# Sparse attention and a top-2 mixture of experts: queries and keys laid out head dimension first, inputs as contiguous blocks, a third PSUM bank for P x V

## The chip, the core and the metric

The kernel runs on one core of one Trainium2 chip. A core has five engines that work side by side and wait for each other by semaphores: PE (TensorE, matmuls; its weight loads are shown as PEld), DVE (VectorE), ACT (ScalarE), POOL (GpSimd) and SP (SyncE, which here only issues DMAs). PE writes into PSUM, which has eight banks of 128 x 512 float32. The metric is device time in microseconds, the median of several runs. Host work in `kernel()` ahead of the launch is not in it.

## What is computed

```python
def _attn_ref(q, k, v, n_sink, window):              # 4 batches, 8 heads, 768 tokens, head dimension 64
    scores = scale * np.matmul(q, k.transpose(0, 1, 3, 2))
    is_sink = pos[None, :] < int(n_sink)             # n_sink = 4
    rel = pos[:, None] - pos[None, :]
    in_window = (rel >= 0) & (rel < int(window))     # window = 128
    scores = np.where(is_sink | in_window, scores, -1000000000.0)
    a = np.exp(scores - np.max(scores, axis=-1, keepdims=True))
    a = a / (np.sum(a, axis=-1, keepdims=True) + 1e-09)
    return np.matmul(a, v)

def _moe_ref(x, w_gate, w_noise, noise, w1, w2):     # 3072 tokens of 512, 8 experts of 1024
    noisy_logits = x @ w_gate + np.log1p(np.exp(x @ w_noise)) * noise
    top2 = np.argpartition(-noisy_logits, 2, axis=1)[:, :2]
    top2_w = ...
    for e in range(E):
        for k in range(2):
            mask = top2[:, k] == e
            h = np.maximum(x[mask] @ w1[e], 0.0)
            out[mask] += top2_w[mask, k, None] * (h @ w2[e])
```

Attention's output, 512 wide per token, is the x of the mixture.

## The kernel before

The program has two phases, and each is recorded into a planner (`Plan`) before it is built. Every piece of work is entered with its engine, a duration, a priority and the tiles that it reads and writes. `Plan.run` then plays the list through: each engine takes, of the pieces that are ready, the one with the smallest priority, and the order that comes out is the order in which each engine's instructions are built. Priorities are a tile number plus offsets from the table `PR`; other entries of `PR` choose engines (`dv_pool`, `pc_pool`, `cm_pool`). Rings (`plan.rings`) say how many buffers of a kind there are; a piece waits until the buffer of its number minus the ring's size is free. SP's DMA issues form one queue in the built order.

Phase one (L1186) is attention with routing woven in. 16 pairs of heads (`g`) with 3 tiles of 256 queries (`jj`) each make 48 tiles `n = 3 g + jj`. Per pair, `load_qk` (L259) brings keys and queries with tokens on partitions (`kn`, `qn`), in runs of 64 floats; for the first pair in three parts, later in one part of two DMAs each. `turn` (L276) lets PE transpose two key and two query blocks of 128 tokens (L280) into the PSUM tile `T`, `turn_c` (L286) copies it with ACT into `kq`, and `ksink` (L290) lets POOL copy the four sink keys beside each key block. `load_v` (L267) brings the values, and `dv` (L271, built by the helper at L192) takes the difference of neighbouring value blocks, on POOL for one pair in four and on DVE for the others.

Per tile: `qk` (L307) writes scores into `S`; ACT copies the previous key block (L310) and DVE merges the current one under a mask (L315, L317) into `cbuf`; DVE takes the maximum (L327), POOL subtracts it (L192), ACT takes exp (L334), DVE sums (L337) and inverts (L345). `ptr` (L365) transposes the probabilities on PE into `P`, ACT copies them to `CT` (L368), POOL or DVE masks them to `CM` (L377, L375). `pv` opens a PSUM tile `X`: a transpose of the sinks' probabilities (L382), values times `CT` (L388), differences times `CM` (L391); ACT copies the sinks' part (L395), `sinks` adds it (L400), ACT copies the result (L408), `rows` transposes it into the same `X` (L413), and DVE scales it into `xr` (L416), which SP stores to `x_rows` (L423). One X tile is thus in use from L382 to L416. The sinks' values come by 16 small DMAs per batch (L247) into a tile that POOL has cleared (L241). `logits` (L593, L601) and `routing` of a finished batch take X tiles of the same ring.

PSUM in phase one: `S` two tiles of two banks, `P` one, `T` one, `X` two. `T` serves the first expert's rows as well (L881). Phase two runs the last batch's routing and the experts: `up` (L997 to L999) and `down` (L1026 to L1032) on PE, weights by `w_chunk` (L918) through the tile `st`, `gather` on POOL, results added into `out` by POOL (L1050).

Of the kernel before, what the change touches and what calls it, by code (L numbers as in the profile page):

```python
# [9 lines left out]
F32 = mybir.dt.float32  # L10
# [29 lines left out]
def dram(t, off, ap):  # L40
    return bass.AP(tensor=t.tensor, offset=t.offset + off, ap=ap)
# [135 lines left out]

def constants(nc, pool, sh):
# [16 lines left out]
def attention(tc, plan, consts, cst, sh, q, k, v, xbuf):  # L195
# [6 lines left out]
    plan.rings.update(vr=2, kn=2, qn=2, vn=2, dv=2, skn=2, sqn=2, kq=2, C=5, mn=3, sm=4, ri=2, pc=3,  # L202
                      CT=2, CM=2, ps=3, xr=3, S=2, P=1, T=1, X=2, xtn=5, lt=1, lm=1, lg=2)
# [71 lines left out]

    def turn(g, gi, ti):  # L276
        p = get("T", ti, [128, 4, 128], F32, "ps")
        for x, nm in enumerate(("kn", "qn")):
            for a in range(2):
                nc.tensor.transpose(p[:, 2 * x + a, :], get(nm, g)[:, 2 * gi + a].rearrange("p h d -> p (h d)"), idf)  # L280

    def kq(g):
        return get("kq", g, [128, NJ, 4, KW])

    def turn_c(g, gi, ti):
        nc.scalar.activation(kq(g)[:, gi, :, NS:], get("T", ti), AF.Copy)  # L286

    def ksink(g, gi):
        t = kq(g)
        nc.gpsimd.tensor_copy(t[:, gi, :2, :NS], t[:, 0, 0:1, NS:2 * NS].to_broadcast([128, 2, NS]))  # L290
# [140 lines left out]
    def load(nm, g, gi, z):  # L431
        plan.dma(z, lambda: load_qk(nm, g, gi), 1.9 if gi is None else .65, w=[(nm, g, i) for i in parts(gi)], u=[(nm, g)], n=2)

    def parts(gi):
        return range(NJ) if gi is None else (gi,)

    def turns(g, gi, z):
        ti = plan.next("T")
        op("PE", .43, z + P(g, "tgroup"), lambda: turn(g, gi, ti), r=[(nm, g, gi) for nm in nms], w=[("T", ti)], u=[(nm, g) for nm in nms])
        op("ACT", .49, z + P(g, "tgroup_c"), lambda: turn_c(g, gi, ti), r=[("T", ti)], w=[("kq", g, gi)], u=[("kq", g)])  # L440
        op("Pool", .14, z + P(g, "ksink"), lambda: ksink(g, gi), r=[("kq", g, 0), ("kq", g, gi)], w=[("ks", g, gi)], u=[("kq", g)])
# [13 lines left out]
    for g in range(NP):  # L455
        p0 = g * NJ
        e = p0 - NJ
        for nm in nms:
            if g:
                load(nm, g, None, (g - 3) * NJ + PR.get("load_qk", 0) + 1.5 * (nm == "qn") if g > 1 else -18)  # L460
        if g:
            loads_v(g)
        for gi in range(NJ):
            turns(g, gi, e + PR.get("t0", .8) + PR.get("t2", .4) * gi)
            if g == 0 and gi == 0:
                plan.op("SP", 0, -19, None, r=[("kq", 0, 0), ("ks", 0, 0)], w=[("go", 0)], lat=0)
        if g == 0:
            loads_v(0)
# [9 lines left out]
        for jj in range(NJ):  # L478
# [31 lines left out]
            op("PE", .14, n + .6 + P(g, "sinks"), lambda n=n: sinks(n), r=[("ps", n), ("vr", g // HP)], w=[("X", xa)], kind=3)  # L510
# [8 lines left out]
def routing_setup(nc, pool, tmp, cst, sh, w_gate, w_noise, noise):  # L519
# [4 lines left out]
    wbd = c["wbd"] = tmp.tile([128, HP, 2, 2, E], F32, name="wbd")  # L524
    nc.gpsimd.memset(wbd, 0.0)
# [40 lines left out]
def gate_loads(nc, plan, cst, sh, w_gate, w_noise, noise):  # L566
    c, wbd = cst, cst["wbd"]
    D, E, HP, T = sh.D, sh.E, sh.H // 2, sh.T

    def load():  # L570
        for h in range(2):
            for i, w in enumerate((w_gate, w_noise)):
                nc.sync.dma_start(wbd[h * D:(h + 1) * D, :, h, i, :], dram(w, h * D * E, [[E, D], [2 * D * E, HP], [1, E]]))
        nc.sync.dma_start(c["nz"], dram(noise, 0, [[E, 128], [128 * E, T], [1, E]]))

    c["gates"] = lambda: plan.dma(2, load, 4, r=[("xrow", 0)], w=[("rc", 0)], n=5)
# [341 lines left out]
def w_chunk(plan, nc, sh, w1, w2, e, m, i, z, lo_eng="DVE", first=()):  # L918
# [4 lines left out]
    quarters = m == 1 and e > 0  # L923

    def load():
        t = get("st", n, [128, 1024], F32, "early")
        if m == 1:
            t = t.rearrange("p (k f) -> p k f", k=4)
            o = e * sh.DM * sh.F + i * 256
            if quarters:  # L930
                for q in range(4):
                    nc.sync.dma_start(t[32 * q:32 * q + 32], dram(w1, o + q * 128 * sh.F, [[sh.F, 32], [32 * sh.F, 4], [1, 256]]))
            else:
                nc.sync.dma_start(t, dram(w1, o, [[sh.F, 128], [128 * sh.F, 4], [1, 256]]))
        else:
# [367 lines left out]
```

## Time and profile before

| What | Value |
|---|---|
| Runs before | 839.18 us median of 3 (837.86 to 840.2) |
| Span of the profiled execution | 836.0 us (the page gives no time of it beside the span) |
| Granted TensorE clock, mean | 0.990 |
| DMA | 97.10 MB in 151750 packets, 100704 of them under 512 B |
| First H matmul of the experts | 226.89 us from the start |

The profile is of one execution. A table by stretch gives the busy time of each engine between two times; a row of the timeline gives start, length, engine, line and operation, with the idle time ahead of it and what ended that in brackets; a row of groups gives an operation's count, its busy time and mean length, and the idle time just ahead of it; a row of waits gives the total, the number of times and the longest. Most fp32 matmuls appear as two records each, transposes as one.

### The profile page before, as it was taken

What the parts mean: (1) busy time and instruction counts of PE and PEld (TensorE: products, weight loads), DVE (VectorE), ACT (ScalarE), POOL (GpSimd) and SP (SyncE); (2) the same over time, 40 slices, a digit from 0 to 9 for tenths busy, and PEclk for the clock granted to TensorE, in tenths of its full rate; (3) what the DMA queues carried; (4) which work ended last, traced back from release to release, by engine and by line L of the source; (5) the groups of instructions that cost most, each with busy time, mean ns of one, the idle gap of its engine ahead of it and who ended that gap; (6) DMA issues with size and microseconds to landing.
All of it is one profiled execution on the core that took longest, in us unless ns stands there. A gap on an engine that the chain in (4) does not pass through costs nothing.

```text
span 836.0 us, 13410 instructions
## 1 busy us (share of the span) xinstructions
PE 794.0 (95%) x4801; PEld 668.6 (80%) x4801; DVE 442.8 (53%) x1094; ACT 343.5 (41%) x677; POOL 430.3 (51%) x601
## 2 busy tenths in 40 slices
PE   6999997898899799999999999999999999999996
PEld 3776775676677589888988988898899889889984
DVE  5878979888673334346335424633542463454220
ACT  4876785675521323234233323423332341433210
POOL 6555866767416325472753647275364627526212
PEclk9999999999999899999999999999999999999999
DMA  6749886644544186175444617544461654444123
GB/s 120 154 96 226 181 204 183 157 127 100 141 132 131 31 224 165 29 152 120 94 84 127 136 31 153 122 92 84 129 131 35 150 124 94 80 130 78 21 31 47
DMA packets 151750, 97.10 MB, mean 116 GB/s; under 512 B 100704, under 2 KB 129376, under 8 KB 151680
## 3 DMA queue, kind: packets, MB, share of 16 engines
q1 hardware_dynamic: 137744, 67.93, 31.8%
q0 software_dynamic: 13936, 28.27, 19.4%
q8 instruction: 39, 0.64, 0.3%
q14 instruction: 31, 0.25, 0.1%
HBM read 67.44 MB, written 28.72 MB: 115 GB/s over the span
## 4 chain that ended last, share of the span: by engine, by line
PE 75%; issue 7%; DVE 6%; POOL 4%; DMA 4%; ACT 2%; another core or an unknown queue 1%; SPq 1%; POOLq 0%; DVEq 0%; ACTq 0%
PE H L997 10%; PE H L999 10%; PE H L998 10%; PE Y L1026 9%; PE Y L1028 9%; PE Y L1027 9%; PE S L307 4%; PE X L388 2%; PE T L280 2%; PE X L391 2%; POOL out L1050 2%; PE P L365 1%; PE Y L1031 1%; PE Y L1032 1%; DMA st<-in_moe_w 1%
## 5 line engine op out<-in xcount | busy, mean ns | idle before, releaser
L1050 POOL DMA_INDIRECT out<-y,idx x56 | 92.0, 1642 | 241.2 <-ACT y L1035 209.3
L838 POOL DMA_INDIRECT xg<-x_rows,rt_idq x182 | 180.6, 992 | 55.5 <-issue 53.4
L1015 DVE SCALAR_TENSOR_TENSOR h<-H,h 128x384 fp32r<-128x384 f32 (+2 forms) x192 | 79.4, 441 | 219.6 <-ACT h L1008 142.2
L997 PE MATMUL H<-skn,w 128*128 128x448 f32 (+3 forms) x512 | 181.6, 355 | 1.8 <-issue 1.8
L999 PE MATMUL H<-skn,w 128*128 128x448 f32 (+3 forms) x512 | 180.5, 353 | 1.5 <-issue 1.5
L998 PE MATMUL H<-sqn,w 128*128 128x448 f32 (+3 forms) x512 | 179.3, 350 | 1.8 <-issue 1.8
L1008 ACT ACTIVATE h<-H 128x448 fp32r<-128x448 f32 (+3 forms) x128 | 66.1, 516 | 273.7 <-PE H L999 161.8
L997 PEld LDWEIGHTS H<-skn,w 128*128 128x128 f32 x512 | 96.2, 188 | 11.2 <-issue 3.1
L998 PEld LDWEIGHTS H<-sqn,w 128*128 128x128 f32 x512 | 96.3, 188 | 10.6 <-issue 2.4
L999 PEld LDWEIGHTS H<-skn,w 128*128 128x128 f32 x512 | 96.3, 188 | 7.3 <-issue 1.8
L1026 PE MATMUL Y<-w2b,h 128*128 128x512 f32 x192 | 76.0, 396 | 0.3 <-ACT h L1008 0.2
L1028 PE MATMUL Y<-w2b,h 128*128 128x512 f32 x192 | 75.5, 393 | 0.5 <-DVE h L1015 0.5
L1026 PE MATMUL Y<-w2a,h 128*128 128x512 f32 x192 | 75.5, 393 | 0.0
L1027 PE MATMUL Y<-w2b,h 128*128 128x512 f32 x192 | 75.5, 393 | 0.0
L1027 PE MATMUL Y<-w2a,h 128*128 128x512 f32 x192 | 75.0, 391 | 0.0
L1028 PE MATMUL Y<-w2a,h 128*128 128x512 f32 x192 | 74.8, 389 | 0.0
L307 PE MATMUL S<-kq 64*128 64x264 f32 (+1 forms) x384 | 57.4, 410 | 4.4 <-DVE cbuf L317 2.5
L192 POOL TENSOR_TENSOR cbuf<-cbuf,mn 128x528 f32<-128x528 f32 x48 | 51.7, 1077 | 18.4 <-DVE mn L327 16.4
L895 ACT ACTIVATE skn<-xtn 128x512 fp32r<-128x512 f32 (+1 forms) x49 | 29.4, 600 | 68.0 <-DVE xtn L886 55.3
L1028 PEld LDWEIGHTS Y<-w2b,h 128*128 128x128 f32 x192 | 36.3, 189 | 9.9 <-DVE h L1015 1.7
L307 PEld LDWEIGHTS S<-kq 64*128 64x128 f32 x384 | 31.4, 192 | 15.6 <-issue 4.8
L192 DVE TENSOR_TENSOR sqn<-xtn,skn 128x512 fp32r<-128x512 f32 (+1 forms) x49 | 31.9, 652 | 22.1 <-ACT skn L895 16.0
(191 smaller groups left out, 1362.7 us busy)
## 6 DMA issues: line engine op xcount, KB each, us to landing
st<-in_moe_w SPq DMA_DIRECT2D x36, 512.0 KB
st<-in_moe_w SPq DMA_DIRECT2D x112, 128.0 KB
out<-zt SPq DMA_DIRECT2D x31, 256.0 KB
vn<-in_v SPq DMA_DIRECT2D x16, 384.0 KB
x_rows<-xr SPq DMA_DIRECT2D x48, 128.0 KB
kn<-in_k SPq DMA_DIRECT2D x30, 192.0 KB
qn<-in_q SPq DMA_DIRECT2D x30, 192.0 KB
xg<-x_rows,rt_idq POOLq DMA_INDIRECT x182
```

Of the source, the lines that this page charges most:

```text
L192: eng.tensor_tensor(out, a, b, op=OP.subtract)
L307: nc.tensor.matmul(p[:, :2 if j else 1], kq(g)[r, j // 2, 2 + j % 2, NS:], x[:, :2 if j else 1], start=True, stop=True)
L838: nc.gpsimd.indirect_dma_start(out=x[:, i, :], out_offset=None, in_=xbuf.rearrange("r (q d) -> (r q) d", d=sh.SW), in_offset=bass.Indirect ...
L997: nc.tensor.matmul(p, w[:, 0, i], xh, start=(i == 0), stop=False)
L998: nc.tensor.matmul(p, w[:, 0, i], xl, start=False, stop=False)
L999: nc.tensor.matmul(p, w[:, 1, i], xh, start=False, stop=(i == DC - 1))
L1008: nc.scalar.activation(get("h", FC * q + f, [128, 2 * 128 * FIRST], F32R)[:, :width], get("H", FC * q + f), AF.Relu)
L1015: nc.vector.scalar_tensor_tensor(h[:, o:o + s1 - s0], p[:, s0:s1], 0.0, h[:, s0:s1].bitcast(F32), op0=OP.max, op1=OP.subtract)
L1026: nc.tensor.matmul(p, hh, w[:, 0], start=(f == 0), stop=False)
L1027: nc.tensor.matmul(p, hh, w[:, 1], start=False, stop=False)
L1028: nc.tensor.matmul(p, hl, w[:, 0], start=False, stop=(f == FC - 1))
L1050: d = nc.gpsimd.indirect_dma_start(out=out, out_offset=bass.IndirectOffsetOnAxis(ap=c["idx"][:size(e, t), e, t:t + 1], axis=0), in_=get("y ...
```

## The change

`kernel()` lays the inputs out anew on the host, in a new function `laid_out`: keys and queries of a pair with head dimension first, the sink keys already beside each block, as one block per pair; values, sinks' values (with their zeros), gate weights, noise and expert weights each as the block that one DMA brings. On the device the transposes `turn`, the copies `turn_c` and `ksink`, the clearing of the sinks' tile and the tiles `kn`, `qn` and `T` are gone; `kq` has a ring of three instead of two. The bank of `T` becomes a third `X` bank, which also takes the first expert's rows. The numbers in `PR` are all new; of the entries that choose engines, `dv_pool` goes from 1 to 3 and `pc_pool` from 4 to 2. Some durations given to the planner change.

```diff
-PR = dict(dv_pool=1, cm_pool=11, gap=1.5, pc_pool=4, warm=1, cur=11.119, cur1=0.687, cur1_0=44.511, cur1_9=-33.328,
...
+PR = dict(dv_pool=3, cm_pool=11, gap=1.5, pc_pool=2, warm=1, cur=0.024, cur1=1.512, cur1_0=-2.463, cur1_9=-0.944,
...
+KQ, PB, XB = 3, 1, 3
...
+def laid_out(np, sh, q, k, v, w_gate, w_noise, noise, w1, w2):
...
+    turned = lambda x: x.reshape(NP, 2, S, D).transpose(0, 1, 3, 2).reshape(NP, 128, NJ, 2, 128)
+    kt = turned(k)
+    qk_t = np.zeros((NP, 128, NJ, 4, 128 + NS), np.float32)
+    qk_t[:, :, :, :2, :NS] = kt[:, :, :1, :1, :NS]
+    qk_t[:, :, :, :2, NS:] = kt
+    qk_t[:, :, :, 2:, NS:] = turned(q)
+    values = v.reshape(NP, 2, NB, 128, D).transpose(0, 3, 1, 2, 4)
...
+    first = w1[:1].reshape(1, 4, 128, 4, 256).transpose(0, 3, 2, 1, 4)
+    others = w1[1:].reshape(E - 1, 4, 4, 32, 4, 256).transpose(0, 4, 1, 3, 2, 5)
...
-    plan.rings.update(vr=2, kn=2, qn=2, vn=2, dv=2, skn=2, sqn=2, kq=2, C=5, mn=3, sm=4, ri=2, pc=3,
-                      CT=2, CM=2, ps=3, xr=3, S=2, P=1, T=1, X=2, xtn=5, lt=1, lm=1, lg=2)
+    plan.rings.update(vr=2, vn=2, dv=2, skn=2, sqn=2, kq=KQ, C=5, mn=3, sm=4, ri=2, pc=3,
+                      CT=2, CM=2, ps=3, xr=3, S=2, P=PB, X=XB, xtn=5, lt=1, lm=1, lg=2)
...
-    def sink_zero(b):
-        nc.gpsimd.memset(vs(b), 0.0)
...
+        nc.sync.dma_start(get("st", vst[b], [128, 1024], F32, "early"), vsink[b])
...
-    def turn(g, gi, ti):
-        p = get("T", ti, [128, 4, 128], F32, "ps")
-        for x, nm in enumerate(("kn", "qn")):
-            for a in range(2):
-                nc.tensor.transpose(p[:, 2 * x + a, :], get(nm, g)[:, 2 * gi + a].rearrange("p h d -> p (h d)"), idf)
-
-    def turn_c(g, gi, ti):
-        nc.scalar.activation(kq(g)[:, gi, :, NS:], get("T", ti), AF.Copy)
-
-    def ksink(g, gi):
-        t = kq(g)
-        nc.gpsimd.tensor_copy(t[:, gi, :2, :NS], t[:, 0, 0:1, NS:2 * NS].to_broadcast([128, 2, NS]))
...
+    def load_kq(g, gi):
+        t, s = kq(g).rearrange("p g x k -> p g (x k)"), 4 * KW
+        if gi is not None:
+            nc.sync.dma_start(t[:, gi], qk_t[g, :, gi * s:(gi + 1) * s])
+        else:
+            nc.sync.dma_start(t.rearrange("p g y -> p (g y)"), qk_t[g])
 
     def load_v(g):
-        nc.sync.dma_start(get("vn", g, [128, 2, NB, D]),
-                          dram(v, g * 2 * S * D, [[D, 128], [S * D, 2], [128 * D, NB], [1, D]]))
+        nc.sync.dma_start(get("vn", g, [128, 2, NB, D]).rearrange("p h b d -> p (h b d)"), v[g])
...
-            op("PE", 1.0 if jj else .78, n + .6 + P(g, "pv"), lambda n=n: pv(n),
+            op("PE", 1.12 if jj else .9, n + .6 + P(g, "pv"), lambda n=n: pv(n),
...
+        nc.sync.dma_start(get("st", n, [128, 1024], F32, "early"), (w1 if m == 1 else w2)[e, i])
...
-        rows_turn(plan, nc, cst, sh, 0, t, 128, "T", PR.get("gt", 48))
+        rows_turn(plan, nc, cst, sh, 0, t, 128, "X", PR.get("gt", 48))
```

Two places show what this does to the order. The first is PE's queue early in attention (in the second and third pair before), where `S` are scores, `P` probabilities, `X` the tiles of P x V with their buffer's number, `T` the transposes of keys and queries. Before:

```order
L307 MATMUL S_600<-kq_430 128x264 x2
L400 MATMUL X_559<-ps_596,vr_369 128x128 x2
L413 MATMUL X_525<-idf_66,xtn_569 128x128 x2
L365 MATMUL P_615<-idf_66,cbuf_143 128x128 x4
L413 MATMUL X_559<-idf_66,xtn_569 128x128 x2
L280 MATMUL T_625<-idf_66,kn_467 128x128 x2
L280 MATMUL T_625<-idf_66,qn_489 128x128 x2
L307 MATMUL S_635<-kq_430 128x264 x2
L365 MATMUL P_643<-idf_66,cbuf_143 128x128 x4
L280 MATMUL T_651<-idf_66,kn_467 128x128 x2
L280 MATMUL T_651<-idf_66,qn_489 128x128 x2
L382 MATMUL X_662<-idr_68,pcbuf_145 128x128
```

Now, at about the same place in the second pair:

```order
L407 MATMUL X_403<-ps_426,vr_186 128x128 x2
L389 MATMUL X_441<-idr_68,pcbuf_144 128x128
L395 MATMUL X_441<-CT_411,vn_165 64x128 x4
L398 MATMUL X_441<-CM_416,dv_277 64x128 x4
L389 MATMUL X_461<-idr_68,pcbuf_144 128x128
L395 MATMUL X_461<-CT_437,vn_165 64x128 x4
L398 MATMUL X_461<-CM_457,dv_277 64x128 x4
L314 MATMUL S_477<-kq_167 128x264 x2
L314 MATMUL S_485<-kq_167 128x264 x2
L407 MATMUL X_441<-ps_471,vr_186 128x128 x2
L407 MATMUL X_461<-ps_480,vr_186 128x128 x2
L420 MATMUL X_403<-idf_66,xtn_453 128x128 x2
```

The four L280 rows are gone, and tiles X_441 and X_461 are opened ahead of the last write into X_403 (L420), so three X tiles are in use at once where before the third, X_662, came behind the last write into both others.

The second place is the start of SP's queue, where `kn`, `qn`, `kq`, `vn` and `st` are the tiles that the DMAs fill (`st` holds the sinks' values here). Before:

```order
L264 DMA kn<-in_k 128x2x64 x2
L264 DMA qn<-in_q 128x2x64 x2
L264 DMA kn<-in_k 128x2x64 x2
L264 DMA qn<-in_q 128x2x64 x2
L264 DMA kn<-in_k 128x2x64 x2
L264 DMA qn<-in_q 128x2x64 x2
L264 DMA kn<-in_k 128x6x64 x2
L268 DMA vn<-in_v 128x12x64 x2
L264 DMA qn<-in_q 128x6x64 x2
L247 DMA st<-in_v 4x4x64 x16
```

Now:

```order
L287 DMA kq<-in_qk_t 128x528
L292 DMA vn<-in_v 128x768
L270 DMA st<-in_vsink 128x1024
L287 DMA kq<-in_qk_t 128x528 x2
L289 DMA kq<-in_qk_t 128x1584
L292 DMA vn<-in_v 128x768
```

One block brings the first part of the first pair's keys and queries; values and sinks' values stand ahead of its second and third part. SP's whole queue has 179 rows now and had 206.

More of the change, by code (lines that the diff above doesn't have):

```diff
@@ L192, in minus, with attention @@
     eng.tensor_tensor(out, a, b, op=OP.subtract)
-def attention(tc, plan, consts, cst, sh, q, k, v, xbuf):
+def attention(tc, plan, consts, cst, sh, qk_t, v, vsink, xbuf):
     nc = tc.nc
@@ L429, in attention, with load @@
     XA = {}
[L431 to L441, printed above, removed]
+    def load(g, gi, z):
+        plan.dma(z, lambda: load_kq(g, gi), 3.8 if gi is None else 1.3, w=[("kq", g, i) for i in (range(NJ) if gi is None else (gi,))],
+                 u=[("kq", g)])
     def loads_v(g):
-        plan.dma((g - 1) * NJ + PR.get("load_v", 1), lambda: load_v(g), 2.2, r=[("go", 0)] if g < 2 else (), w=[("vn", g)])
+        plan.dma((g - 1) * NJ + PR.get("load_v", 1), lambda: load_v(g), 1.9, w=[("vn", g)])
     op("Pool", 1.7, -1000, None)
     op("DVE", 2.4, -1000, None)
-    nms = ("kn", "qn")
     for gi in range(NJ):
-        for nm in nms:
-            load(nm, 0, gi, -20 + gi)
+        load(0, gi, -2000 + 6 * gi)
     for i in range(PR.get("warm", 16)):
@@ L457, in attention @@
         e = p0 - NJ
-        for nm in nms:
-            if g:
-                load(nm, g, None, (g - 3) * NJ + PR.get("load_qk", 0) + 1.5 * (nm == "qn") if g > 1 else -18)
         if g:
+            load(g, None, (g - 3) * NJ + PR.get("load_qk", 0) if g > 1 else -1980)
             loads_v(g)
[L463 to L468, printed above, removed]
+        else:
+            plan.dma(-1998, lambda: load_v(0), 1.9, w=[("vn", 0)])
         if g % HP == 0:
             b, z = g // HP, (g - HP) * NJ if g else -6
-            op("Pool", 1.0, z, lambda b=b: sink_zero(b), w=[("st", vst[b])])
-            plan.dma(z, lambda b=b: sink_values(b), .9, r=[("go", 0)], w=[("st", vst[b])], n=16)
+            plan.dma(z if g else -1996, lambda b=b: sink_values(b), 2.2, w=[("st", vst[b])])
             z += 9 if g else 0
@@ L484, in attention @@
                 s = 2 * n + a
-                need = [jj] if not jj or a else [jj - 1, jj]
+                need = {max(jj - 1, 0), jj} if not a else {jj}
                 op("PE", .5 if jj or a else .3, z + P(g, "qk"), lambda n=n, a=a: qk(n, a),
-                   r=[("kq", g, jj)] + [(t, g, i) for t in ("kq", "ks") for i in need], w=[("S", s)], u=[("kq", g)], kind=1)
+                   r=[("kq", g, i) for i in sorted(need)], w=[("S", s)], u=[("kq", g)], kind=1)
                 if jj or a:
@@ L523, in routing_setup @@
     c = cst
-    wbd = c["wbd"] = tmp.tile([128, HP, 2, 2, E], F32, name="wbd")
-    nc.gpsimd.memset(wbd, 0.0)
+    c["wbd"] = tmp.tile([128, HP, 2, 2, E], F32, name="wbd")
     exact = dict(allow_small_or_imprecise_dtypes=True)
@@ L563, in routing_setup, with gate_loads @@
     nc.vector.tensor_scalar(c["spare"], c["slot"], float(sh.N), None, op0=OP.add)
-def gate_loads(nc, plan, cst, sh, w_gate, w_noise, noise):
+def gate_loads(nc, plan, cst, sh, w_gates, noise):
     c, wbd = cst, cst["wbd"]
-    D, E, HP, T = sh.D, sh.E, sh.H // 2, sh.T
     def load():
[L571 to L576, printed above, removed]
+        nc.sync.dma_start(wbd.rearrange("p g h i e -> p (g h i e)"), w_gates)
+        nc.sync.dma_start(c["nz"].rearrange("p t e -> p (t e)"), noise)
+    c["gates"] = lambda: plan.dma(2, load, 2.5, r=[("xrow", 0)], w=[("rc", 0)], n=2)
 def logits(nc, plan, cst, sh, b, jj, z):
@@ L922, in w_chunk @@
     key, pool = w_tile(plan, m, e, i)
-    quarters = m == 1 and e > 0
     def load():
[L926 to L935, printed above, removed]
-            nc.sync.dma_start(t.rearrange("p (a d) -> p a d", a=2),
-                              dram(w2, (e * sh.F + i * 256) * sh.DM, [[sh.DM, 128], [128 * sh.DM, 2], [1, sh.DM]]))
+        nc.sync.dma_start(get("st", n, [128, 1024], F32, "early"), (w1 if m == 1 else w2)[e, i])
     def hi():
@@ L944, in lo @@
         minus(nc.vector if lo_eng == "DVE" else nc.gpsimd, t[:, 1], get("st", n), t[:, 0].bitcast(F32))
-    plan.dma(z, load, 1.8 if m == 1 else 1.5, r=first, w=[("st", n)], n=4 if quarters else 1)
+    plan.dma(z, load, 2.2, r=first, w=[("st", n)])
     plan.op("ACT", .95, z, hi, [("st", n)], [key])
@@ L1183, in zero, with phase_one @@
              .73, r=r, w=[("zero", i)])
-def phase_one(tc, nc, plan, ac, tail, cst, sh, q, k, v, w1, w2, xbuf, out):
+def phase_one(tc, nc, plan, ac, tail, cst, sh, qk_t, v, vsink, w1, w2, xbuf, out):
     NT = sh.S // 128
@@ L1203, in go_on @@
                 todo[0][0] = n + PR.get("gap", 2)
-    for n in attention(tc, plan, ac, cst, sh, q, k, v, xbuf):
+    for n in attention(tc, plan, ac, cst, sh, qk_t, v, vsink, xbuf):
         go_on(n)
@@ L1277, in moe_kernel @@
         p2.count["st"] = plan.count["st"]
-        phase_two(tc, nc, p2, cst, sh, w1, w2, xbuf, out)
+        phase_two(tc, nc, p2, cst, sh, w1c, w2c, xbuf, out)
         p2.run()
```

80 lines of the change are left out of this document (41 added, 39 removed).

## The prediction

> **What bounds the kernel now.** I read the page's head first, then a table of busy time by stretch.
>
> ```profile
> span 836.0 us, 13410 instructions
> PE 794.0 (95%) x4801; PEld 668.6 (80%) x4801; DVE 442.8 (53%) x1094; ACT 343.5 (41%) x677; POOL 430.3 (51%) x601
> ```
>
> TensorE is busy 95% of the span, but that average mixes attention (to about 226 us) with the experts behind it. The table by stretch gives, after start, end and length, the busy time of PE, weight load, DVE, ACT and POOL, then granted clock, DMA share and GB/s.
>
> ```profile
> 21.00:63.00 42.00, 40.46 (x375) 30.21 (x373) 34.50 (x77) 33.84 (x82) 24.47 (x52) 1.00 0.62 126
> 63.00:84.00 21.00, 19.06 (x188) 13.81 (x186) 17.17 (x58) 14.58 (x39) 11.02 (x25) 1.00 0.92 224
> 84.00:105.00 21.00, 20.48 (x211) 15.96 (x210) 20.81 (x58) 16.46 (x42) 16.95 (x33) 1.00 0.82 184
> 105.00:126.00 21.00, 20.95 (x203) 15.35 (x203) 16.20 (x37) 17.35 (x41) 13.69 (x28) 1.00 0.85 207
> 126.00:150.00 24.00, 18.51 (x189) 13.75 (x187) 22.67 (x67) 13.19 (x37) 17.71 (x30) 1.00 0.62 153
> 150.00:185.00 35.00, 32.31 (x308) 23.85 (x305) 27.92 (x59) 25.72 (x62) 24.21 (x39) 0.95 0.66 168
> 185.00:205.00 20.00, 17.11 (x166) 12.48 (x162) 17.80 (x64) 9.42 (x29) 15.43 (x35) 0.91 0.34 82
> 290.00:836.00 546.00, 537.14 (x2606) 476.96 (x2604) 229.21 (x516) 175.71 (x273) 260.13 (x276) 1.00 0.48 102
> ```
>
> Attention has two kinds of stretch. In 21-63, 63-84, 105-126 and 150-185 (119 us) PE is busy 112.8 us, 95%, and DVE 95.8 us, 80.5%. In 84-105, 126-150 and 185-205 (65 us), where routing of a finished batch runs on DVE, DVE is busy 61.3 us, 94%, and PE 56.1. So PE sets the pace in 119 us and DVE in 65. From 290 us on PE is busy 98% with expert matmuls, which the change leaves alone.
>
> Is PE really full in the first kind? Busy time of pipelined matmuls can hide slack, so I read start-to-start times in the timeline (start, length).
>
> ```profile
> 109.28 0.62 PE L365 MATMUL P<-idf,cbuf 128*128 128x128 f32 x4
> 109.74 0.38 PE L280 MATMUL T<-idf,kn 128*128 128x128 f32 x2
> 109.96 0.38 PE L280 MATMUL T<-idf,qn 128*128 128x128 f32 x2
> 110.18 0.38 PE L413 MATMUL X<-idf,xtn 128*128 128x128 f32 x2
> ```
>
> Each row starts before the one ahead of it has ended: PE takes new work as fast as it can, and a pair of transposes holds the queue 0.22 us. The Trainium skill, page "Perfetto Trace Analysis", section "Identifying the Most-Contended Engine", says that matmul busy time is a poor measure of this engine and that weight-load busy time is better. By that rule 105-126 is only 15.35 of 21, 73%, full, and the removal would bring about what the first rival below gives. The starts above speak against it here.
>
> **The change, part by part.** *Transposes (L280, L286, L290).* A group of two keys and two queries holds PE from 109.74 to 110.18, 0.44 us. The table for line 280 alone counts them:
>
> ```profile
> 21.00:63.00 42.00, 7.87 (x52) 5.54 (x50) 1.00 0.62 126
> 63.00:84.00 21.00, 3.71 (x24) 2.72 (x24) 1.00 0.92 224
> 105.00:126.00 21.00, 4.83 (x32) 3.46 (x31) 1.00 0.85 207
> 150.00:185.00 35.00, 4.26 (x28) 3.23 (x28) 0.95 0.66 168
> ```
>
> That is 136 transposes, 34 groups, 15.0 us of PE time in the PE-bound stretches. What stands on the other engines:
>
> ```profile
> L280 PE MATMUL T<-idf,kn 128*128 128x128 f32 x96 | 19.7, 288 | 2.1 <-ACT kq L286 1.2 <-DMA kn<-in_k 0.9
> L286 ACT ACTIVATE kq<-T 128x512 f32<-128x512 f32 x48 | 28.6, 595 | 8.8 <-PE T L280 7.4 <-PE S L307 1.2
> L290 POOL COPY kq<-kq 128x8 f32<-128x8 f32 x48 | 9.3, 205 | 4.1 <-ACT kq L286 4.0
> L192 DVE TENSOR_TENSOR dv<-vn 128x640 f32<-128x640 f32 x12 | 13.0, 1080 | 0.6 <-DMA vn<-in_v 0.6
> L192 POOL TENSOR_TENSOR dv<-vn 128x640 f32<-128x640 f32 x4 | 6.2, 1547 | 2.1 <-DMA vn<-in_v 2.1
> L356 ACT ACTIVATE pcbuf<-cbuf 128x32 fp32r<-128x32 f32 x24 | 5.5, 229 | 0.1
> ```
>
> ACT loses 28.6 us and takes 12 more small copies (pc_pool 4 to 2), 12 x 0.229 = 2.7. It was not the bound, so I count nothing for it; PE's matmuls and DVE's reductions cover it, and were that cover gone it could only give. *Value differences (dv_pool 1 to 3).* Eight of DVE's 12 `dv` go to POOL: DVE loses 8 x 1.08 = 8.7 us, POOL gains 8 x 1.547 = 12.4 and loses the 9.3 of L290. Spread evenly over the 205 us from 21 to 226, DVE loses 8.7 x 119/205 = 5.0 us where PE binds and 8.7 x 65/205 = 2.8 where DVE binds.
>
> **Sum for PE-bound stretches.** With 15.0 us of PE gone, DVE is the next late one: it still has 95.8 - 5.0 = 90.8 us there. If it can be filled no better than now (80.5%), the stretches last 90.8/0.805 = 112.8 us, a gain of 6.2. If PE alone decides, the gain is 15.0, with DVE at 87%, still under the 94% that it reaches where it binds. I take 85%, nearer the second end because DVE's own stretches show 94%: 90.8/0.85 = 106.8, a gain of **12.2 us** (6.2 to 15.0). **In DVE-bound stretches** PE's saving is hidden and the moved `dv` gives **2.8** (0 to 2.8).
>
> That move has a counter-effect. In the timeline a routing step on DVE with two operands in SBUF stood beside a POOL subtraction:
>
> ```profile
> 135.24 2.37 POOL L192 TENSOR_TENSOR w<-st,w 128x1024 fp32r<-128x1024 f32 x1
> 135.62 2.06 DVE L678 TENSOR_TENSOR rt_ln<-rt_ln,nz 128x48 f32<-128x48 f32 x1
> 138.22 0.19 DVE L679 TENSOR_TENSOR rt_no<-lg,rt_ln 128x48 f32<-128x48 f32 x1
> ```
>
> L678 ended at 137.68, just behind POOL's 137.61, and took 2.06 us where a step of its size took 0.19. Eight more POOL subtractions of 1.55 us can hold up such steps; at half a row each that is 6 us, if every one met one. I take none, since L290's 48 POOL copies go away, and leave the 2.8 open down to 0. The Trainium skill, page "SBUF — State Buffer", section "Who interferes with whom", states the lock: a VectorE instruction with two SBUF inputs and a GpSimd instruction that reads SBUF exclude each other. The trace agrees by L678; by this rule alone the 2.8 would shrink.
>
> *Third X bank.* Who waited on PE's queue:
>
> ```profile
> PE X L382 <- DVE xr L416: 4.2, 3, 2.1
> PE X L593 <- DVE xr L416: 2.1, 2, 1.5
> ```
>
> L382 opens a new X tile and waits until `xr` has emptied the tile two back; three waits, 4.2 us. Of L593's waits the one of 1.5 lies in attention. A third bank takes the place of the T bank and can end 4.2 + 1.5 = 5.7 us, and can't cost any, since the same matmuls run; as one of them (2.1) came while DVE itself was late, I take **3.5** (0 to 5.7). The next late thing is again DVE.
>
> *Start.* The first loads become one contiguous block, and no transposes, copies or sink memset stand ahead of the first scores.
>
> ```profile
> 5.94 0.15 DVE L224 TENSOR_SCALAR bit<-biti 128x1 f32<-128x1 int32 x1
> 7.21 2.69 PE L307 MATMUL S<-kq 64*128 64x132 f32 x12
> 8.07 0.43 DVE L315 TENSOR_TENSOR cbuf<-S,m 128x256 f32<-128x256 f32 x1 [1.98 <-PE S L307]
> ```
>
> Scores started at 7.21 and DVE's first mask at 8.07, after 1.98 us of waiting; DVE's constants end at 6.09. So the gain stops at **2.0**; the second block of keys now stands behind values and sinks on SP and may come as much later, so the other end is -2.0. I take 2.0, because DVE has the first tile to work on meanwhile.
>
> *Loads.* q, k, v, weights and gates become whole blocks; SP issues 27 rows fewer. In the experts PE's matmuls hide the weight loads, 537.1 of 546 us, so I count 0; with that cover gone or bettered, the 8.9 us of PE's idle time there is what could move.
>
> Sum: 12.2 + 2.8 + 3.5 + 2.0 = 20.5; 836.0 - 20.5 = 815.5 us of span. The page gives no time of its own execution; the runs' median of 839.18 lies 3.2 above the span, and I keep that: **818.7 us**.
>
> **Rivals.** *A: DVE binds.* PE had slack and DVE stays at 80.5%: 6.2 + 2.8 = 9.0, no bank or start gain, 830.2 us. For it: the second engine is close behind; against it: the 94%. *B: everything comes.* 15.0 + 2.8 + 5.7 + 2.0 = 25.5, and a slow stretch behind attention goes too:
>
> ```profile
> 272.64 0.40 PE L999 MATMUL H<-skn,w 128*128 128x512 f32 x1 [0.44 <-issue]
> 274.04 0.39 PE L997 MATMUL H<-skn,w 128*128 128x512 f32 x1 [1.00 <-issue]
> ```
>
> Six matmuls there start 1.4 us apart instead of 0.23, 7 us lost to no wait that the profile names. Without it 32.5 are gained, 806.7 us; if it doubles, the forecast loses 7. *C: slower, by one late load.* A pair's queries and keys now land as one block of 0.81 MB, and no score of the pair can start before. SP takes its queue in order, behind stores that wait:
>
> ```profile
> SPq L423 <- DVE xr L416: 32.0, 13, 6.2
> 151.30 5.05 DMA vn<-in_v
> ```
>
> A block behind the longest such wait (6.2), landing at twice the 5.05 us of the 0.39 MB of values, comes 16.6 us after its turn. With a ring of three it has two pairs' time, six tiles of 206/48 = 4.3, about 26 us. The point is a turn over 9 us late; if each of 13 blocks then held PE 2 us, 26 - 20.5 = 5.5 us are lost: 844.7. *D: it doesn't do what it says*: the new numbers reorder every engine and lose what the transposes gave, 839.
>
> **How the numbers follow.** Forecast 818.7: 0.50, its own bounds 812 to 827. A 0.20, B 0.20, C 0.04, D 0.06. The range reaches over A and B and leaves C and D out: 805 to 832. About 0.3%, 2.5 us, is what a measurement of this kernel can tell from no change: faster 0.90, same 0.06, slower 0.04.
>
> **What would show it.** Attention's last X projection ahead of the first H matmul falls from 226 to about 206 us; the former PE-bound stretches show DVE at 85% or more; L382's waits for `xr` are gone; the first mask is near 6.1. Attention ending at 217 with DVE at 80% means A; PE waiting for `kq` from a DMA means C. The forecast fails if the order of the new numbers leaves PE and DVE waiting for each other more than the 6.2 and 8.9 us that PE idles in the two kinds of stretch now.

## The result, and the profile after

| | before | after |
|---|---|---|
| Runs | 839.66 us median of 4 (837.86 to 840.2) | 816.75 us median of 4 (815.94 to 818.95) |
| Ratio, 95% interval | | 0.9742 (0.9713 to 0.9771): faster |
| Span of the profiled execution | 836.0 us | 815.5 us (817.08 us for the whole execution) |
| First H matmul of the experts | 226.89 us | 201.08 us |
| From there to the end of the span | 609.1 us | 614.4 us |

The forecast was 818.7 us (805 to 832). Attention became 25.8 us shorter, where 20.5 were forecast, and the experts, for which nothing was forecast, 5.3 us longer. The two errors cancel, which is luck. The right total hides both, and most of the experiments are about them.

The head of the page of the changed kernel, then the prediction's table by stretch (start, end, length; busy time of PE, weight load, DVE, ACT and POOL; granted clock, DMA share, GB/s):

```profile
span 815.5 us, 12512 instructions
PE 777.9 (95%) x4609; PEld 651.9 (80%) x4609; DVE 437.1 (54%) x1086; ACT 320.6 (39%) x641; POOL 428.2 (53%) x544
```

```profile
21.00:63.00 42.00, 41.32 (x396) 29.96 (x392) 37.44 (x90) 32.52 (x87) 27.20 (x45) 1.00 0.61 184
63.00:84.00 21.00, 18.77 (x183) 13.54 (x175) 20.86 (x70) 12.26 (x35) 14.77 (x28) 0.92 0.52 164
84.00:105.00 21.00, 21.00 (x224) 15.51 (x222) 19.80 (x48) 15.44 (x42) 16.73 (x25) 1.00 0.78 213
105.00:126.00 21.00, 17.05 (x162) 12.16 (x158) 20.24 (x49) 15.32 (x41) 17.37 (x23) 0.99 0.66 213
...
150.00:185.00 35.00, 30.06 (x312) 21.57 (x313) 33.43 (x98) 20.99 (x58) 29.19 (x51) 1.00 0.41 113
```

VectorE is now nearly level with TensorE: 37.44 of 42 us in the first stretch (89%), and above TensorE in 63-84, 105-126 and 150-185. By this view alone VectorE would be the new bound. What TensorE's queue waits for (total, times, longest, in us):

```profile
PE S L314 <- DVE cbuf L324: 6.8, 5, 3.0
...
PE S L314 <- DMA kq<-in_qk_t: 3.8, 2, 2.9
...
PE X L389 <- DVE xr L423: 0.2, 1, 0.2
```

Opening an X tile (L389, before the change L382) waits 0.2 us for `xr`, where it waited 4.2. The scores (L314) wait for VectorE's merge now, and once 2.9 us for the second block of keys. The start, in the timeline (start, length, and the idle time ahead with what ended it):

```profile
3.74 1.69 PE L314 MATMUL S<-kq 64*128 64x132 f32 x8 [0.88 <-DMA kq<-in_qk_t]
8.35 2.13 PE L314 MATMUL S<-kq 64*128 64x264 f32 x8 [2.92 <-DMA kq<-in_qk_t]
...
3.14 0.26 DVE L236 TENSOR_SCALAR le<-nz 128x128 uint8<-128x128 int32 x1
3.27 0.22 DVE L238 TENSOR_SCALAR ge<-nz 128x128 f32<-128x128 int32 x1
...
4.60 0.43 DVE L322 TENSOR_TENSOR cbuf<-S,m 128x256 f32<-128x256 f32 x1 [0.39 <-PE S L314]
```

The first mask stands at 4.60 us instead of 8.07, earlier than the 6.1 that the prediction took for its limit.

### The profile page after: what moved, and what is told of

It is laid out like the page before. It is cut to its first block, busy times and chain, and to the rows that moved or that the text cites. A ratio compares the mean times of both kernels' runs of the same rounds, so it can differ in the third digit from the quotient of the medians.

```text
span 815.5 us, 12512 instructions
## 1 busy us (share of the span) xinstructions
PE 777.9 (95%) x4609; PEld 651.9 (80%) x4609; DVE 437.1 (54%) x1086; ACT 320.6 (39%) x641; POOL 428.2 (53%) x544
## 4 chain that ended last, share of the span: by engine, by line
PE 70%; issue 7%; DVE 7%; POOL 6%; DMA 4%; ACT 3%; another core or an unknown queue 1%; SPq 1%; POOLq 0%; DVEq 0%; ACTq 0%
PE H L971 10%; PE H L973 10%; PE H L972 10%; PE Y L1000 9%; PE Y L1002 9%; PE Y L1001 9%; PE S L314 3%; PE X L395 2%; PE P L372 2%; POOL out L1024 2%; PE Y L1005 1%; PE Y L1006 1%; POOL cbuf L221 1%; POOL xg L824 1%; PE X L398 1%
## 5 line engine op out<-in xcount | busy, mean ns | idle before, releaser
L1000 PE MATMUL Y<-w2b,h 128*128 128x512 f32 x192 | 77.7, 405 | 5.0 <-issue 3.8
L1002 PE MATMUL Y<-w2b,h 128*128 128x512 f32 x192 | 76.8, 400 | 0.5 <-DVE h L989 0.5
L1001 PE MATMUL Y<-w2b,h 128*128 128x512 f32 x192 | 76.6, 399 | 0.0
L314 PE MATMUL S<-kq 64*128 64x264 f32 (+1 forms) x384 | 59.9, 424 | 12.6 <-DVE cbuf L324 6.8
L314 PEld LDWEIGHTS S<-kq 64*128 64x128 f32 x384 | 33.9, 199 | 27.7 <-DVE cbuf L324 10.0
L1000 PEld LDWEIGHTS Y<-w2b,h 128*128 128x128 f32 x192 | 36.6, 191 | 14.0 <-issue 5.8
L1002 PEld LDWEIGHTS Y<-w2b,h 128*128 128x128 f32 x192 | 36.6, 191 | 10.6 <-DVE h L989 2.1
```

What stands on the lines that cost most here:

```text
L314: nc.tensor.matmul(p[:, :2 if j else 1], kq(g)[r, j // 2, 2 + j % 2, NS:], x[:, :2 if j else 1], start=True, stop=True)
L1000: nc.tensor.matmul(p, hh, w[:, 0], start=(f == 0), stop=False)
L1001: nc.tensor.matmul(p, hh, w[:, 1], start=False, stop=False)
L1002: nc.tensor.matmul(p, hl, w[:, 0], start=False, stop=(f == FC - 1))
```

## The experiments

The runs went to several chips, on which the kernel before took 839.15 us (e1 to e4), 837.29 (e5 to e8), 827.96 (e9, e11, e13) and 825.44 (e12, the same chip as e9). So kernels are compared by their ratio to it, and their stretches by the trace. "Attention" is the start of the first H matmul, "experts" the time from there to the start of the last expert matmul.

| Kernel | us, median | ratio to before (95%) | attention | experts |
|---|---|---|---|---|
| before | 839.66 | 1 | 226.9 | 600.7 |
| after | 816.75 | 0.9742 (0.9713 to 0.9771) | 201.1 | 606.1 |
| e1 w2b at its old place | 812.25 | 0.9693 (0.9668 to 0.9719) | 201.8 | 600.4 |
| e2 weights from rows | 815.16 | 0.9720 (0.9694 to 0.9747) | 201.4 | 606.3 |
| e3 two X banks | 836.21 | 0.9969 (0.9945 to 0.9993) | 220.1 | 607.9 |
| e4 dv on VectorE | 816.92 | 0.9751 (0.9719 to 0.9783) | 199.1 | 603.2 |
| e5 transposes put back | 843.88 | 1.0064 (1.0041 to 1.0088) | 225.9 | 608.4 |
| e6 old numbers, three banks | 824.94 | 0.9848 (0.9805 to 0.9891) | 209.6 | 606.5 |
| e7 old numbers, two banks | 831.74 | 0.9941 (0.9915 to 0.9967) | 216.0 | 606.3 |
| e8 keys first | 814.43 | 0.9728 (0.9698 to 0.9758) | 202.7 | 602.2 |
| e9 skn moved | 805.27 | 0.9727 (0.9713 to 0.9742) | 201.9 | 594.9 |
| e11 w2b moved, clearing | 808.71 | 0.9767 (0.9749 to 0.9786) | 202.7 | 596.4 |
| e12 keys first, new order | 806.13 | 0.9762 (0.9736 to 0.9788) | 204.5 | 591.8 |
| e13 e1 and e4 together | 799.81 | 0.9660 (0.9640 to 0.9681) | 197.1 | 591.6 |

### Where the experts lost 5.3 us: e1 and e2

The loss is a drift, 0.5 us at the experts' second piece and 5.3 at the end. In the timeline the H matmuls keep their distance (203.6 and 203.8 ns from start to start for 448 columns, before and after), but the Y matmuls that read `w2b` went from 229.9, 227.9 and 230.8 ns (their three lines) to 235.7, 233.0 and 236.1; those that read `w2a` moved by 1.3 ns at most. Two things differ there: the weights come as blocks, and `w2b` is allocated behind `lg` now, 384 bytes higher in SBUF, because the planner happens to build `lg` first. No other tile of the experts moved.

```diff
     def total():
+        if last:
+            plan.rings["w2b"] = 2
+            get("w2b", 0, [128, 2, 1024], F32R, "sb")
         nc.vector.tensor_reduce(get("lg", b, [128, NT, 2 * E])[:, 2 * jj:2 * jj + 2, :],
```

> The changed kernel with one difference in the experts' tiles: w2b stands 384 bytes lower in SBUF, where it stood before the change, and lg behind it instead of ahead of it. Theory 1 (the 5.3 us given back in the experts come from w2b's place): the down projection's matmuls that read w2b, 235.7, 233.0 and 236.1 ns from start to start now, fall to about the 229.9, 227.9 and 230.8 of before; some 640 matmuls by 5.5 ns give 3.5 us, so 813 us. Theory 2 (the weights' new blocks in DRAM and their shorter loads disturb TensorE): the place does nothing, 235 ns stay, 816.7 us within 1.

e2, in `w_chunk`:

```diff
-        nc.sync.dma_start(get("st", n, [128, 1024], F32, "early"), (w1 if m == 1 else w2)[e, i])
+                    nc.sync.dma_start(t[32 * q:32 * q + 32], dram(w1, o + q * 128 * sh.F, [[sh.F, 32], [32 * sh.F, 4], [1, 256]]))
...
+                              dram(w2, (e * sh.F + i * 256) * sh.DM, [[sh.DM, 128], [128 * sh.DM, 2], [1, sh.DM]]))
```

> The changed kernel with the expert weights loaded from their rows as before the change (runs of 1 and 2 KB, four DMAs for most blocks of w1), w2b at its new place. Theory 1 (w2b's place): the w2b matmuls stay at 235 ns, 816.7 us, or up to 1 us more for the longer loads. Theory 2 (the new blocks): they fall to about 229 ns and the time to 813.

Nine neighbouring matmuls on `w2b`, the first and the last of them, in the timeline of the changed kernel:

```profile
400.96 0.40 PE L1000 MATMUL Y<-w2b,h 128*128 128x512 f32 x1
...
402.83 0.39 PE L1002 MATMUL Y<-w2b,h 128*128 128x512 f32 x1
```

and in that of e1:

```profile
399.09 0.39 PE L1003 MATMUL Y<-w2b,h 128*128 128x512 f32 x1
...
400.90 0.39 PE L1005 MATMUL Y<-w2b,h 128*128 128x512 f32 x1
```

Eight steps take 1.87 us after (234 ns each) and 1.81 in e1 (226). Over all pieces from 300 us on, e1's three lines measure 228.3, 227.6 and 228.0 ns, e2's 234.4, 233.1 and 235.3. The experts take 600.4 us in e1, as before the change, and 606.3 in e2, and every run of e1 (811.29 to 814.32 us) is below every run of e2 (814.55 to 817.65) on the same chip. So the place of `w2b` costs time, and the blocks in DRAM cost nothing. By the pace, 640 matmuls at 5.4 ns more than before the change make 3.5 us of the 5.3; the medians put e1 2.9 us below e2 and 4.5 below the changed kernel. The rest isn't shown to come from the place: the experts' first piece alone, in which a stretch of low clock varies from run to run (see rival B at the end), took 58.0 us after the change and 56.1 in e1. The view of groups shows the place inside one kernel, by the mean length of a matmul from 300 to 790 us after the change:

```profile
L1000 PE MATMUL Y<-w2b,h 128*128 128x512 f32 x157 | 62.4, 397 | 0.3
...
L1000 PE MATMUL Y<-w2a,h 128*128 128x512 f32 x157 | 61.4, 391 | 0.0
```

### Which place is slow: e9, and e11's first half

```diff
+    plan.get("pad", 0, [128, 32], F32, "early")
     both = [plan.get(nm, i, [128, 4, 128 * FIRST], F32R, "early") for nm in ("skn", "sqn")]
+    plan.get("pad2", 0, [128, 96], F32, "early")
```

> As e1, and the tiles skn and sqn, which the H matmuls read, stand 128 bytes higher in SBUF; all tiles behind them stand 512 bytes higher. In e1 the tiles that are read fast (w2a, w2b) begin 32 bytes behind a multiple of 256, and the slow place of w2b began 160 bytes behind one, as skn and sqn do. Theory (that remainder sets the pace): the H matmuls, 203.6 ns for 448 columns and 175.5 for 384, get 2 to 5 ns shorter, about 1500 x 3 = 4.5 us less, 808 us. Rival (the remainder is nothing, w2b's trouble was of another kind): 203.6 ns stay, 812.25 us within 1.

e11 has a `pad` of 128 bytes ahead of `w2b` and, at the start:

```diff
+    clear = consts.tile([128, 2, 1024], F32, name="clear")
+    for i in range(2):
+        nc.gpsimd.memset(clear[:, i], 0.0)
```

> Two changes far apart in time, read from the trace, each in its own stretch. (a) w2b stands 128 bytes above its place in e1, so again 160 bytes behind a multiple of 256, but not at its slow place. Theory (the remainder of 256 sets the pace): its matmuls take 233 to 236 ns, as at the slow place. Rival (only the exact place, or the remainder of 512): 228 ns, as in e1. (b) At the start GpSimd clears two unused blocks of 128x1024, as it did before the change. Theory (the clearing held up VectorE's masks): le and ge take about 2.0 us again instead of 0.26 and 0.22, and VectorE's constants end near 6 us instead of 4.2. Rival (they were held up by something else): 0.26 and 0.22.

`w2b` at 128 bytes above its good place was slow again: 233.2, 232.6 and 232.0 ns. That agrees with the remainder of 256, but e9 doesn't: with `skn` and `sqn` at the good remainder, H matmuls of 448 columns took 202.4 ns instead of 203.7, and those of 384 columns 175.7 instead of 175.4, far from the 2 to 5 ns expected. Worse, the second and third line of the Y matmuls on `w2a`, which had not moved, went from 227.6 and 226.0 ns in e1 to 230.6 and 231.7. What had moved is `h`, their other operand, by 512 bytes like all tiles behind `skn` and `sqn`. So the place of a tile counts, and not of the moving operand alone; the rule behind it stays open.

### Is TensorE still the bound? e5

```diff
             nc.tensor.matmul(p[:, :2 if j else 1], kq(g)[r, j // 2, 2 + j % 2, NS:], x[:, :2 if j else 1], start=True, stop=True)
+        for h in range(2):
+            nc.tensor.transpose(get("S", 2 * n + a)[:, h, 2 * KW:2 * KW + 128], kq(g)[:, j // 2, 2 + h, NS:], idf)
```

> The changed kernel with TensorE's old work put back and nothing else: behind each pair of score matmuls two transposes of 128x128 from kq into columns of S that nobody reads, 192 in all as before the change, 48 x 0.44 = 21.1 us of TensorE. The order of all other work is kept, no copy and no wait is added. Theory (the prediction's term: in the stretches that TensorE bounds, the transposes gave 12.2 us, at most 15.0): 12 to 15 us more, 829 to 832 us. Rival (VectorE is the fuller engine now, and TensorE's 18.9 us of idle time in attention hide them): 0 to 5 us more, 817 to 822 us.

Attention became 24.8 us longer, all but 1.0 of what the change had gained there. That is more than either theory said, because the dummies cost more than I reckoned. In e5's timeline two pairs stand so, the first holding TensorE 0.37 us up to the next start, the second 0.19:

```profile
106.42 0.44 PE L316 MATMUL S<-idf,kq 128*128 128x128 f32 x2
106.79 0.72 PE L314 MATMUL S<-kq 64*128 64x264 f32 x4
107.44 0.44 PE L316 MATMUL S<-idf,kq 128*128 128x128 f32 x2
107.63 0.64 PE L409 MATMUL X<-ps,vr 128*128 128x128 f32 x4
```

Summed from start to start over all of attention, the 192 dummies hold TensorE 30.2 us (157 ns each; those of L280 held it 22.3, 118 each), and the scores between them 5.6 us more than after the change. With small losses elsewhere TensorE's work grew by 33.1 us, from 177.7 to 210.8, and its idle time fell from 18.9 to 10.2. So three quarters of the added work (24.8 of 33.1) show in the time, although VectorE looked fuller. By the same share the 22.3 us of L280 are worth 16.7. TensorE is still the bound for most of attention, with a cover of some 9 us. One part stays mixed: the dummies also hold back the copies out of S, and no run put them elsewhere.

### Bank and numbers: e3, e6 and e7

```diff
-KQ, PB, XB = 3, 1, 3
+KQ, PB, XB = 3, 1, 2
```

> The changed kernel with a ring of two X banks, the eighth bank left empty. Theory (the third bank is worth what the prediction said): 3.5 us more, 820.2 us (816.7 to 822.4), and L389, which opens an X tile, waits 3 to 6 us for xr again. Rival (VectorE sets the pace now, so the bank is hidden): 816.7 us within 1.

e6 and e7 take `PR` as it was before the change, `dv_pool` and `pc_pool` excepted; e7 has `XB = 2` as well.

> The changed kernel with the priorities in PR as before the change; dv_pool, pc_pool and the three X banks stay. Theory 1 (the third bank pays only with an order that uses it): the order falls back towards the two banks', 10 us more or over, 827 to 836 us. Theory 2 (layout and bank pay by themselves): 817 to 820 us.

> The changed kernel with the priorities in PR as before the change and two X banks: the layout and the moved dv alone. By the prediction's terms without the bank 839.2 - 12.2 - 2.8 - 2.0 = 822 us, less than 5 us slower than with three banks and the same numbers. If the bank is worth some 19 us whatever the numbers are, it is 836 us or more, and as much slower than with three banks.

Attention in a table of two by two (before the change it was 226.9):

| | two X banks | three X banks |
|---|---|---|
| old numbers | 216.0 (e7) | 209.6 (e6) |
| new numbers | 220.1 (e3) | 201.1 (after) |

With the old numbers, the change without the bank (layout, loads, a third `kq`, moved dv and sinks' copies) is worth 10.9 us, and the bank 6.4. With the new ones the bank is worth 19.0. The new numbers give 8.5 us with three banks and lose 4.1 with two. e3's 836.21 us lie above both values that were expected, and e7's 831.74 between its two; e6's 824.94 come near the first of its theories. The new numbers were found for a third bank: with two, TensorE stands before tiles that are not yet free. The row of waits of e3:

```profile
PE X L389 <- DVE xr L423: 10.1, 9, 3.7
```

That is over twice the 4.2 of before. The other waits of e3 name no row of that size; its idle time on TensorE is 28.8 us, against 18.9 after. The rest of the 19.0 us lies in TensorE's own work, 187.1 against 177.7 us from start to start for the same matmuls in another order, and no wait names it. A part is the granted clock, which averages 0.96 over e3's attention and 0.97 over the changed kernel's; over 220.1 and 201.1 us that is some 3 us more lost in e3. e3's own runs go with the clock too, from 830.31 us at 0.985 to 839.41 at 0.972. Whether the order brings the lower clock wasn't tried.

### Values' differences: e4 and e13

```diff
-PR = dict(dv_pool=3, cm_pool=11, gap=1.5, pc_pool=2, warm=1, cur=0.024, cur1=1.512, cur1_0=-2.463, cur1_9=-0.944,
+PR = dict(dv_pool=1, cm_pool=11, gap=1.5, pc_pool=2, warm=1, cur=0.024, cur1=1.512, cur1_0=-2.463, cur1_9=-0.944,
```

> The changed kernel with dv_pool=1: eight of the 12 value differences go back from GpSimd to VectorE, 8 x 1.06 = 8.5 us more on VectorE. Theory (VectorE is now the fuller engine in attention): 2.8 us more from the stretches with routing and up to 8.5 in all, 819.5 to 825.2 us. Rival (what GpSimd's subtractions hold up on VectorE costs as much): 816.7 us within 1.

> e1 and e4 together: w2b at its old place and dv_pool=1. If the move of dv to GpSimd gave what the prediction says (2.8 us), 815 us; if it cost 2 us, as the first H matmul of e4 at 199.1 us against 201.1 says, 810.3 us; if nothing, 812.25.

Eight `dv` more on VectorE, and attention ended 2.0 us earlier in e4, and 4.8 earlier in e13 than in e9 on the same chip. The total of e4 is no different from after (0.9751 against 0.9742, intervals overlapping); e13 stands below e9 (0.9660 against 0.9727, apart), of which the Y matmuls of e9 took a part. Nor are the 4.8 us all from `dv`: the granted clock averages 0.99 over attention in e13, but 0.97 in e9, e4 and the changed kernel, and e13 ends attention, which it shares with e4, 2.0 us earlier than e4. Against e1, from which it differs by `dv` alone, e13's ratio is 0.0033 lower, 2.8 us, with intervals that overlap. And e4's trace is of the fastest of its four runs (812.32 us; the others took 816.15 to 818.68). So the gain is 2 to 3 us in the traces, and the totals don't tell it from nothing. Why VectorE doesn't mind shows in its groups during attention (count, busy time, mean ns). After the change:

```profile
L331 DVE TENSOR_TENSOR cbuf<-cbuf,m 128x8 f32<-128x8 f32 x16 | 8.7, 544 | 0.1
...
L221 DVE TENSOR_TENSOR dv<-vn 128x640 f32<-128x640 f32 x4 | 4.6, 1139 | 0.0
...
L665 DVE TENSOR_TENSOR rt_no<-lg,rt_ln 128x48 f32<-128x48 f32 x3 | 2.7, 902 | 0.0
```

and in e4:

```profile
L221 DVE TENSOR_TENSOR dv<-vn 128x640 f32<-128x640 f32 x12 | 11.0, 915 | 0.0
...
L331 DVE TENSOR_TENSOR cbuf<-cbuf,m 128x8 f32<-128x8 f32 x16 | 5.2, 324 | 0.1
...
L665 DVE TENSOR_TENSOR rt_no<-lg,rt_ln 128x48 f32<-128x48 f32 x3 | 1.4, 453 | 0.1
```

Tiny steps with two operands in SBUF take up to twice as long where GpSimd has more subtractions: 544 ns for 128x8 values, which are 8 a lane, against 324, and 902 against 453 for L665. The move saved VectorE 6.4 us of `dv`, and the sum of all its groups in attention is 207.6 us after against 202.9 in e4. So part of what made VectorE look full were held-up steps. That agrees with what the Trainium skill, page "SBUF — State Buffer", section "Who interferes with whom", says of such pairs: a VectorE instruction with two inputs in SBUF contends with a GpSimd instruction that reads SBUF. Whether the gain of e4 comes from this or from subtractions that no longer queue behind `dv` on GpSimd, the runs don't tell.

### The start: e8, e12, and e11's second half

In e8 the planner's order is kept, and only the two loads move ahead in SP's queue (e1's edit is in it too):

```diff
+            if self.early:
+                order = [i for i in order if i not in self.early]
+                at0 = next(k for k, i in enumerate(order) if self.ops[i][0] == "SP") + 1
+                order[at0:at0] = self.early
```

> The changed kernel with w2b at its old place, as in e1, and one change in SP's queue alone: the second and third block of the first pair's keys and queries are issued ahead of the first values and sinks' values; every other instruction stays in its place. Theory (TensorE's wait of 2.9 us for the second block at 8.35 us delays all of attention): 1.5 to 2.9 us less than the 812.25 us of e1, 809.4 to 810.8. Rival (VectorE or the later values take its place): 812.25 within 1.

The wait for the key block went, and another took its place. In e8's timeline:

```profile
3.69 3.92 PE L320 MATMUL S<-kq 64*128 64x132 f32 x16 [0.83 <-DMA kq<-in_qk_t]
10.44 1.12 PE L378 MATMUL P<-idf,cbuf 128*128 128x128 f32 x4 [2.84 <-ACT cbuf L347]
...
7.15 1.53 POOL L227 TENSOR_TENSOR dv<-vn 128x640 f32<-128x640 f32 x1 [3.83 <-DMA vn<-in_v]
8.65 1.06 POOL L227 TENSOR_TENSOR cbuf<-cbuf,mn 128x528 f32<-128x528 f32 x1
```

All scores of the first pair's early tiles run at once, but the values land later, `dv` starts at 7.15 us instead of 5.48, GpSimd subtracts the maximum only behind it, and TensorE stands 2.84 us before the probabilities instead of 2.92 before the keys. The sinks' transpose that opens the first X tile comes at 13.88 us, as in e1 (13.83). e12 gives the same loads to the planner, with `dv_pool=1`:

```diff
-        load(0, gi, -2000 + 6 * gi)
+        load(0, gi, -2000 + gi / 2)
```

> e13 with the first pair's second and third block of keys and queries ahead of values and sinks, and this time the planner knows it and orders everything anew. Theory (in e8 the wait went to the late values and to dv ahead of the subtraction on GpSimd, which a new order can mend): 1 to 2 us less than e13, a ratio to before of 0.964. Rival (the numbers in PR fit the order that they were found for, and any new order is worse): a ratio of 0.970 or over.

0.9762, well above e13's 0.9660: attention is 7.4 us longer in the new order (204.5 against 197.1). That the numbers fit only the order that they were found for is the likely reason; it wasn't traced further.

e11's second half: VectorE's constants beside GpSimd's clearing.

```profile
3.14 1.07 DVE L236 TENSOR_SCALAR le<-nz 128x128 uint8<-128x128 int32 x1
3.27 1.00 DVE L238 TENSOR_SCALAR ge<-nz 128x128 f32<-128x128 int32 x1
4.19 1.05 DVE L240 TENSOR_SCALAR m<-nz 128x128 f32<-128x128 int32 x1
5.27 1.48 DVE L242 COPY m<-m 128x4 f32<-128x4 f32 x1
...
3.16 2.00 POOL L254 MEMSET clear<- 128x1024 f32 x2
...
5.20 1.53 POOL L221 TENSOR_TENSOR dv<-vn 128x640 f32<-128x640 f32 x1
```

`le` takes 1.07 us instead of 0.26 and `ge` 1.00 instead of 0.22, less than the 2.0 expected; a copy of four columns takes 1.48 us beside `dv`. The constants end at 7.13 us, against 4.21 after and 6.09 before the change. The clearing held up the first three, the last of which ends with it (5.24 against 5.16 us); the copy behind them was held up by `dv`.

## Why the prediction was right, and where it wasn't

**TensorE binds: right.** The reading of start-to-start times carried. The page "Perfetto Trace Analysis" of the Trainium skill (section "Identifying the Most-Contended Engine") would have TensorE 73% full by its weight loads in 105-126, and rival A with it. The trace agrees in so far as there was a cover of some 9 us (e5), but not with the 830 us of A.

**The transposes, 12.2 us: about right, by another split.** e5's share makes it 16.7 over all of attention, a little above the upper end of 15.0, which counted the TensorE-bound stretches alone. What failed is the step "VectorE is the next late one, and can be filled to 85%": it was filled to 95% in 150-185 (33.43 of 35 us), and its fullness was partly waiting for GpSimd. The split into stretches that one engine bounds was too sharp; in 84-105, put down to VectorE, TensorE had been busy for 20.48 of 21 us.

**The moved dv, 2.8 us: wrong.** It gave nothing that the totals show, and undoing it made attention 2 to 3 us shorter in the traces (e4; the 4.8 of e13 against e9 hold a higher clock as well). The prediction named the counter-effect, at up to 6 us, and took none of it.

**The third bank, 3.5 us: too small.** 6.4 with the old numbers, 19.0 with the new ones, some 3 of these beside a lower clock in e3. The waits of before (5.7 at most) price a bank only for the order of before. Here the order was changed with it, and the two are worth more together than apart.

**The numbers: a missing term.** The prediction had the new order only as a danger (rival D). It gave 8.5 us with three banks.

**The start, 2.0 us: right in size, wrong in its limit.** 6.09 was no limit, since the constants themselves were held up by the clearing that the change removes. The first mask gained 3.47 us, of which 2.6 reached the first X tile (15.92 us before, 13.32 after), as the second block of keys came late, which the prediction had named.

**The experts, 0: wrong.** "The matmuls hide the loads" was true (e2), and beside the point: of the 5.3 us, some 3.5 went because a tile that the change doesn't mention got another place in SBUF (e1).

**The rivals.** C's late block came, but once, at the start, for 2.9 us. The slow stretch that B wanted gone stayed (about 247 to 259 us after the change), and it goes with a drop of the granted clock. The table by stretch has the same 22 us, from 39 us behind the first H matmul, after the change and in e13:

```profile
240.00:262.00 22.00, 16.55 (x67) 12.80 (x66) 6.90 (x22) 4.01 (x8) 9.22 (x11) 0.84 0.14 35
236.00:258.00 22.00, 22.00 (x113) 18.84 (x112) 9.97 (x28) 8.52 (x15) 16.06 (x19) 1.00 0.45 75
```

In 252-259 the clock is 0.51, and from 254.65 us on the Y matmuls start 0.43 us apart instead of 0.23. Before the change it is 0.51 in 276-283, where the last three of the six matmuls 1.4 us apart start (272.64 to 279.67); half a clock does not explain that distance, and it stays open. Ten traces, these two among them, have such a drop, 48 to 52 us behind the first H matmul, and the four from the chip of e9, of four different kernels, have none. In these four the experts' first piece, up to where the H matmuls have 320 columns, took 48.0 to 49.3 us, against 54.9 to 58.7 in the others, and the kernel before is 11 us faster as well. What sets off the drop no run shows.

In sum, the change without bank and new numbers gave 10.9 us of attention (17.0 forecast), the bank 6.4, the numbers 8.5, and the experts took 5.3 back: 20.5, as forecast, from other parts. That these add up to the forecast is luck.

## What to carry to other kernels

A resource and an order that uses it are priced together: measured by itself, the bank looked like 6 us, and with the order found for it like 19. When a phase that nothing touched gets slower, compare the distances of its instructions with those before and then the addresses of its tiles; here an edit of three lines, which moves one tile, brings 812.25 us (0.9693), and with `dv` back on VectorE 0.9660 (intervals overlapping), both below the changed kernel. Before a small difference between two traces is put down to an edit, their granted clocks have to be compared. A full engine isn't the bound until added work on it shows: eight `dv` more on the fuller engine cost nothing, and work on the other one came through at three quarters.

## What the runs showed of the hardware

- A matmul of 128x512 takes 228 or 232 to 236 ns from start to start, depending on where in SBUF the tiles lie (384 or 128 bytes make the difference), with no wait in the trace.
- GpSimd clearing memory stretches VectorE's tensor_scalar from 0.26 to 1.07 us (before the change 2.02), and a GpSimd subtraction a copy of four columns from 0.17 to 1.48.
- A transpose of 128x128 holds TensorE 118 ns in a row of its like, and 157 between score matmuls that use 64 of the rows.
- A drop of the granted clock some 50 us behind the experts' start (0.51 over 7 us after the change) stands in ten traces and in none of the four from the chip of e9, where the experts' first piece takes 48.0 to 49.3 us instead of 54.9 to 58.7.
